# Attention values loaded to stepped partitions of SBUF, and the last strided values loaded into the key tiles

## The chip, the cores and the metric

The kernel runs on 1 core of a Trainium2 chip. The metric is device time of one execution in microseconds (us). TensorE (PE) multiplies, VectorE (DVE), ScalarE (ACT) and GpSimd (POOL) do the rest, and SyncE's queue (SP) issues nearly all transfers, in the order in which they are written.

## The reference

A sparse attention over `q`, `k`, `v` of 8 batches, 8 heads, 576 rows and 64 columns, and a soft mixture of experts behind it:

```
scores = q @ k.T / 8
heads 0..3: keep 0 <= row - key < 32              (local)
heads 4..7: keep key <= row, key % 32 == row % 32 (strided)
x = softmax(scores) @ v, reshaped to 4608 x 512
logits = x @ phi                                  (32 slots)
slot_in  = softmax(logits, over rows).T @ x
slot_out = relu(slot_in @ w1[e]) @ w2[e]          (8 experts, 4 slots each)
out = softmax(logits, over slots) @ slot_out
```

All is float32. The three attention inputs are 28.3 MB, the two weight tensors 33.6 MB, the output 9.4 MB.

## The kernel before

**Sets.** The attention runs over nine sets. Eight are the batches, without their first 64 rows; the set called B gathers those first 64 rows of all batches and is the fifth in order (`SETS`). In a set the four local heads and the four strided heads are handled as pairs: `a` is which pair, `j` which head of the pair. One set is some 60 small steps, each with a name in the text `ASEQ` (lines 38 to 44). An entry such as `AVs0:3` says that in iteration `it` the step is written for set `it - 3`; `A` or `D` behind it puts a copy on ACT or DVE. So ASEQ is a software pipeline five stages deep: with it every engine's order, and the order on SP's queue, are set by hand, and no scheduler changes them.

**Names of steps.** `LKl LQl LKs LQs` load keys and queries of the local and strided heads into the four tiles `ld[x][i]` (512 KB each), `LDr` loads the first key rows into `rest`. `TlK TlQ TsK TsQ Tr` transpose them on PE into PSUM; `lK lQ sK sQ lrK srK` copy them to `kbl`, `ql`, `kbs`, `qs`. `SL`, `SS` are the score products, `mxl`/`mxs` row maxima, `sbl`/`sbs` the subtraction, `exl`/`exs` the exponential, `sml`/`sms` sums and reciprocals, `nms` the scaling of the strided P. `PTl`, `PTs` transpose P; `ePTl`, `ePTs` copy it out of PSUM; `AVl`, `AVs` multiply it with the values; `X`, `XB`, `LG` transpose the result and make logits; `bm dex dT SI acc` fold the set into the running softmax over rows. `W` loads one weight buffer of 512 KB.

**Values.** A product with the values contracts over 128 partitions: both pairs `a` at once, 64 partitions each, and the zeros of the other pair keep them apart. `load_v1` (line 180) fetches the local heads in two transfers, pair 0 to partitions 0 to 63 and pair 1 to 64 to 127, in runs of 256 bytes. `make_v2` (line 202) makes a copy shifted by 32 keys on POOL, in four copies of 32 partitions. `load_vs` (line 190) fetches the strided heads, 32 partitions at 4 or 68 onwards in runs of 4 KB, and 4 more partitions in a small transfer. P is written to match: `(a, key)` down the partitions. Each tile of values exists once, so a load waits until the products of the set before have read it.

**PSUM.** Steps on PE that fill two banks (`T`, `SL`, `SS`, `PT`, `AV`, `X`, `XB`) take turns in three double banks (`pair2`, line 116): a step waits until what stood there three steps earlier has been read.

**The end of the attention.** Of the 64 weight pieces 24 have buffers of their own. The rest go where an attention tile has had its last use (`alias`, line 218; `freed`, line 270), and later into weight buffers that have been multiplied. For the last set (number 8) V1 and VS are written right behind the last `AVl` and `AVs` of set 7 (lines 570 to 592). Behind the attention, `cf` (constants, line 593) is fetched on ACT's queue, then follow slot inputs, the two expert layers (`h`, `so`) and the output (`o`) with its stores.

Of the kernel before, what the change touches and what calls it, by code (L numbers as in the profile page):

```python
# [22 lines left out]
G = 16  # L23
# [9 lines left out]
NWX = 3  # L33
# [13 lines left out]
def shape_constants():  # L47
# [25 lines left out]
    cf = np.concatenate([ident, same, stack, np.ones((128, 1), np.float32)], 1)  # L73
# [4 lines left out]
def tile_sparse_attention_soft_moe(  # L78
# [26 lines left out]
    ident = const.tile([P, 128], F32, name="ident")  # L105
# [44 lines left out]
    pl = fix.tile([P, 16, 64], F32, name="pl")  # L150
    psd = fix.tile([P, 8, 2, 64], F32, name="psd")
# [4 lines left out]
    pt = work.tile([P, 2, 512], F32, name="pt")  # L156
# [4 lines left out]
    for t in (v1, vs, v2, psd, pts):  # L161
        nc.gpsimd.memset(t, 0.0)
# [27 lines left out]
    def load_vs(b):  # L190
        rows = vs.rearrange("p j g d -> p j (g d)")
        for a in range(2):
            if b < B:
# [3 lines left out]
                continue  # L197
            for j in range(2):
                nc.sync.dma_start(out=rows[64 * a + 4:64 * a + NI, j],
                                  in_=v[:, 4 + 2 * a + j, 0:AUX].rearrange("b (i g) d -> b i (g d)", g=G))  # L200

    def make_v2(i):

        a, y = divmod(i, 2)
        r = 64 * a
        if y == 0:
            nc.gpsimd.tensor_copy(out=v2[r + 32:r + 64, a], in_=v1[r:r + 32, a, :, 1:9])  # L207
        else:
            nc.gpsimd.tensor_copy(out=v2[r:r + 32, a], in_=v1[r + 32:r + 64, a, :, 0:8])  # L209
# [8 lines left out]
    alias = [(ld[x][i].rearrange("p a x -> p (a x)"), {("TlK", "TlQ", "TsK", "TsQ")[2 * x + i]})  # L218
# [7 lines left out]
    alias += [(flat(vs, "p j g d -> p (j g d)", x), {f"AVs{y}" for y in range(4)}) for x in (0, 1024)]  # L226
    alias += [(flat(pl, "p g x -> p (g x)", 0), {"PTl"}), (flat(psd, "p g a x -> p (g a x)", 0), {"PTs"})]
# [162 lines left out]
    def row_sub(b, x):  # L390
        m = stats(b, "mx", x)
        if x == 1:
            nc.vector.tensor_tensor(out=probs(1), in0=scores(b, 1), in1=bc(m, NI), op=ALU.subtract)
            return

        nc.vector.tensor_tensor(out=pl.rearrange("p g (r n) -> p g r n", n=TN),
                                in0=bt[b]["sl"].rearrange("p j (g n r) -> p (j g) r n", n=TN, r=8),
                                in1=m.rearrange("p a g -> p (a g)").unsqueeze(2).unsqueeze(3).to_broadcast([P, 16, 8, TN]),
                                op=ALU.subtract)

    def row_exp(b, x):
# [9 lines left out]
    def nms(b):  # L411
        nc.vector.tensor_tensor(out=probs(1), in0=probs(1), in1=bc(stats(b, "rz", 1), NI), op=ALU.mult)

    def PT(b, x):
        ps = bt[b]["pt"] = pair2(f"pt{b}{x}")
        for g in range(8):
            nc.tensor.transpose(out=ps[:, g // 4, 128 * (g % 4):128 * (g % 4) + 128],  # L417
                                in_=(pl[:, 2 * g:2 * g + 2] if x == 0 else psd[:, g]).rearrange("p a k -> p (a k)"), identity=ident)
# [18 lines left out]
    def ePTs(b, a, cp):  # L437

        d = slice(64 * a, 64 * a + 64)
        cp(out=pts[d, a].rearrange("p j g x -> p (j g x)"), in_=bt[b]["pt"][d].rearrange("p j x -> p (j x)"))  # L440

    def AVs(b, e, w):
# [71 lines left out]
    def emit_acc(cols, ps, al):  # L514
# [6 lines left out]
    nc.scalar.dma_start(out=ident, in_=cfd[:, 0:128])  # L521
# [24 lines left out]
        "ePTl": lambda b, cp: cp(out=two(pt, 512), in_=two(bt[b]["pt"], 512)),  # L546
# [23 lines left out]
    after, left = {"AVl": "V1", "AVs": "VS"}, {"AVl": 2, "AVs": 4}  # L570

    done, asked = set(), 0
    for it in range(min(x[1] for x in todo), NV + max(x[1] for x in todo)):
        for name, stage, cp in todo:
            b = it - stage
            if not 0 <= b < NV or b == NV - 1 and name in after.values():
# [5 lines left out]
            if b == NV - 2 and name[:3] in after:  # L582
                left[name[:3]] -= 1
                if not left[name[:3]]:
                    steps[after[name[:3]]](NV - 1)
                    asked += 1
            asked += b == NV - 2 and name == "VS"
            if b == NV - 1:
                done.add(name)
            for x in [x for x in alias if x[1] <= done and asked > 1]:  # L590
                alias.remove(x)
                freed(x[0])
    nc.scalar.dma_start(out=cf, in_=cfd[:, 128:289])
# [148 lines left out]
    def emit_ct(vb):  # L742
# [36 lines left out]
    held = [n for n, x in enumerate(order) if x.tensor in (ld[0][0].tensor, ld[0][1].tensor)]  # L779
# [91 lines left out]
```

## Time and profile before

| | us |
|---|---|
| three runs | 284.42, 287.0, 291.0 (median 287.0) |
| the profiled execution, whole | 285.93 |
| its span, first to last instruction | 284.1 |
| TensorE busy | 232.5 |
| VectorE busy | 170.5 |
| ScalarE busy | 149.6 |
| GpSimd busy | 50.9 |

The span is what the views below divide; 1.8 us of the profiled execution lie outside it. Busy shares are means over a long attention part (to about 215 us) and an expert part, which have different limits.

### The profile page before, as it was taken

Reading aid. Unit: us, or ns where it says so; the run is one execution under the profiler, and the core shown is the slowest. Engines: PE = TensorE matmul, PEld = TensorE weight load, DVE = VectorE, ACT = ScalarE, POOL = GpSimd, SP = SyncE. Lnnn points to the kernel's source line nnn. Section 1 sums busy time; section 2 is a strip of 40 time slices with the busy share of each in tenths; the row PEclk is TensorE's granted clock in tenths of the full one; section 3 lists DMA queues with packets and bytes.
Section 4 is the critical chain, followed back from the end, with each engine's and each line's share of the span. In section 5 each row is a group of like instructions: output and inputs, shape, how many; then the busy total and the mean of one; then the engine's idle time right before and its main releaser. Section 6 shows DMA issues by size and latency. Waiting matters only on the chain.

```text
span 284.1 us, 8914 instructions
## 1 busy us (share of the span) xinstructions
PE 232.5 (82%) x3841; PEld 167.1 (59%) x3841; DVE 170.5 (60%) x309; ACT 149.6 (53%) x270; POOL 50.9 (18%) x48
## 2 busy tenths in 40 slices
PE   7997899899897899899898899971263999999800
PEld 3675686686685777686685677761241523566700
DVE  5389477587485577587576578851022175688810
ACT  3877686585873676865675677441020011277700
POOL 9205023032023032041023023141000020000000
PEclk9999999999999999999999999997586699999975
DMA  7999999797599998989999997899999399999997
GB/s 204 337 228 315 251 205 281 255 252 224 200 183 293 259 232 264 216 205 250 229 197 278 238 165 219 172 389 316 239 266 357 148 267 352 348 353 366 315 350 243
DMA packets 65416, 74.28 MB, mean 261 GB/s; under 512 B 24288, under 2 KB 50272, under 8 KB 65376
## 3 DMA queue, kind: packets, MB, share of 16 engines
q1 hardware_dynamic: 64416, 73.41, 96.1%
q8 instruction: 30, 0.49, 0.8%
q10 hardware_dynamic: 960, 0.30, 0.4%
q14 instruction: 10, 0.08, 0.1%
HBM read 64.26 MB, written 9.44 MB: 259 GB/s over the span
## 4 chain that ended last, share of the span: by engine, by line
PE 39%; DMA 39%; SPq 11%; ACT 2%; DVE 1%; issue 1%; POOL 0%; DVEq 0%; ACTq 0%; POOLq 0%
DMA vs<-in_v_dram 10%; DMA ld<-in_k_dram 9%; DMA rest<-in_k_dram 8%; DMA ld<-in_q_dram 7%; SPq L258 6%; PE h L691 5%; PE so L787 5%; PE as L281 5%; PE t L294 3%; PE o L815 3%; DMA v<-in_v_dram 3%; PE lg L281 3%; PE pt L417 2%; DMA kbl<-in_cf_dram 2%; PE ss L281 2%; PE al L281 2%
## 5 line engine op out<-in xcount | busy, mean ns | idle before, releaser
L294 PE MATMUL t<-ident,ld 128*128 128x128 f32 x288 | 40.9, 279 | 12.4 <-DMA ld<-in_k_dram 6.4
L294 PEld LDWEIGHTS t<-ident,ld 128*128 128x128 f32 x288 | 31.0, 140 | 23.9 <-issue 7.1
L207 POOL COPY v<-v 32x1024 f32<-32x1024 f32 x18 | 18.8, 1044 | 138.2 <-DMA v<-in_v_dram 127.5
L281 PE MATMUL as<-pts,vs 128*64 128x64 f32 x576 | 22.2, 234 | 10.3 <-DMA vs<-in_v_dram 10.3
L281 PEld LDWEIGHTS as<-pts,vs 128*64 128x64 f32 x576 | 19.7, 147 | 13.8 <-issue 13.4
L440 ACT COPY pts<-pt 64x1024 f32<-64x1024 f32 x18 | 18.1, 1007 | 16.7 <-PE pt L417 16.5
L310 ACT COPY kbl<-t 64x512 f32<-64x512 f32 x27 | 15.7, 581 | 17.3 <-PE t L294 17.0
L552 ACT COPY xt<-as 128x512 f32<-128x512 f32 x18 | 9.7, 589 | 25.2 <-PE as L281 25.2
L313 ACT COPY ql<-t 64x512 f32<-64x512 f32 x36 | 20.9, 580 | 3.6 <-PE t L294 2.7
L432 DVE TENSOR_TENSOR xn<-al,rz 128x512 f32<-128x512 f32 x18 | 11.6, 686 | 18.3 <-PE al L281 18.0
L209 POOL COPY v<-v 32x1024 f32<-32x1024 f32 x18 | 20.8, 1157 | 1.5 <-DMA v<-in_v_dram 0.6
L281 PE MATMUL al<-v,pt 128*32 128x128 f32 x576 | 19.9, 275 | 1.2 <-POOL v L207 1.1
L281 PE MATMUL sl<-kbl,ql 128*32 128x128 f32 x576 | 19.9, 276 | 0.1
L300 DVE COPY qs<-t 128x1024 f32<-128x1024 f32 x9 | 11.0, 1222 | 13.6 <-PE t L294 13.6
L303 ACT COPY kbs<-t 64x1024 f32<-64x1024 f32 x18 | 18.1, 1008 | 0.3
L281 PEld LDWEIGHTS al<-v,pt 128*32 128x32 f32 x576 | 15.2, 109 | 5.1 <-issue 3.6
L281 PEld LDWEIGHTS sl<-kbl,ql 128*32 128x32 f32 x576 | 14.8, 110 | 5.2 <-issue 4.9
L388 DVE TENSOR_REDUCE mx<-sl 128x16 f32<-128x1024 f32 x9 | 11.0, 1223 | 10.1 <-PE sl L281 10.1
L545 ACT COPY xt<-x 128x1024 f32<-128x1024 f32 x9 | 9.1, 1012 | 14.9 <-PE x L455 14.9
L478 DVE TENSOR_REDUCE bm<-lg 128x1 f32<-128x128 f32 x9 | 2.6, 284 | 19.3 <-PE lg L281 19.1
L281 PE MATMUL ss<-kbs,qs 128*32 128x72 f32 x576 | 14.0, 234 | 0.0
L281 PE MATMUL lg<-xt,phs 128*32 128x128 f32 x288 | 12.0, 287 | 1.4 <-ACT xt L552 1.4
(164 smaller groups left out, 436.5 us busy)
## 6 DMA issues: line engine op xcount, KB each, us to landing
wb<-in_moe_w_dram SPq DMA_DIRECT2D x41, 512.0 KB
ld<-in_k_dram SPq DMA_DIRECT2D x32, 256.0 KB
ld<-in_q_dram SPq DMA_DIRECT2D x32, 256.0 KB
v<-in_v_dram SPq DMA_DIRECT2D x16, 288.0 KB
vs<-in_v_dram SPq DMA_DIRECT2D x16, 256.0 KB
ld<-in_moe_w_dram SPq DMA_DIRECT2D x4, 512.0 KB
out_dram<-wb SPq DMA_DIRECT2D x4, 512.0 KB
v<-in_moe_w_dram SPq DMA_DIRECT2D x3, 512.0 KB
```

Of the source, the lines that this page charges most:

```text
L207: nc.gpsimd.tensor_copy(out=v2[r + 32:r + 64, a], in_=v1[r:r + 32, a, :, 1:9])
L209: nc.gpsimd.tensor_copy(out=v2[r:r + 32, a], in_=v1[r + 32:r + 64, a, :, 0:8])
L258: nc.sync.dma_start(out=buf, in_=w1[4 * g + e, 128 * c:128 * c + 128, :])
L281: nc.tensor.matmul(out=out, lhsT=lhsT, rhs=rhs, start=start, stop=stop, skip_group_check=True)
L294: nc.tensor.transpose(out=tp[:, a, P * n:P * n + P], in_=src[:, a, P * n:P * n + P], identity=ident)
L303: cp(out=kbs[r, y].rearrange("p n (j r) -> p n j r", j=2)[:, :, :, AR:PN], in_=tv[r].rearrange("p n (r j) -> p n j r", j=2))
L310: cp(out=kbl[d, e, a].rearrange("p n (j r) -> p n j r", j=2)[:, :, :, AR:PN], in_=tp[r, a].rearrange("p (n r j) -> p n j r", n=4, j=2))
L313: cp(out=ql[d, :, 32 * e:32 * e + 32].rearrange("p t (n r) -> p t n r", n=4), in_=tp[r, a].rearrange("p (n t r) -> p t n r", n=4, r=8))
L432: nc.vector.tensor_tensor(out=xn[:, 0].rearrange("p r (a j d) -> p j r a d", a=2, j=2)[:, j], in0=bt[b]["al"][:, j].rearrange("p (r a d) - ...
L440: cp(out=pts[d, a].rearrange("p j g x -> p (j g x)"), in_=bt[b]["pt"][d].rearrange("p j x -> p (j x)"))
L691: nc.tensor.matmul(out=ph[x][32 * e:32 * e + 32, :], lhsT=sit[:, c, 32 * (4 * g + e):32 * (4 * g + e) + 32], rhs=wts[16 * g + 4 * c + e][: ...
L787: nc.tensor.matmul(out=pos[x][32 * e:32 * e + 32, 0:256], lhsT=hts[g][:, c, 32 * e:32 * e + 32], rhs=wt[:, 256 * e:256 * e + 256], start=( ...
```

## The change

- Values of the local heads go to every second partition: pair 0 to 0, 2, 4, ... and pair 1 to 1, 3, 5, ... The partition is then `(key, a)`, and `row_sub` writes P in that order (two halves `sbl0`, `sbl1`, one for each `a`). `make_v2` becomes two copies of 64 partitions.
- Strided values: one transfer for each `j` brings 32 rows of both pairs to 64 even partitions (a row's pair is four partitions on from the row before it), a small one brings the first 4 rows to 8 odd partitions. P gets a compact tile `psc`, and `nms` writes it spread out into `psd` in two instructions. `ePTs` now copies all 128 partitions and multiplies by a 0/1 column (`own_a`), where before it copied 64 into a tile with zeros.
- `ePTl` copies back into `pl`, the tile of P itself; the tile `pt` is gone. The tail has two extra weight buffers, not three.
- The last set's strided values are loaded into `ld[0][0]` and `ld[0][1]`, the key and query tiles of the local heads, as soon as `TlK` and `TlQ` of that set are done. `V1` of the last set still waits for `AVl` of set 7.
- ASEQ is another text: order, stages and ACT/DVE choices differ; SP's loads have other places.

The core of the diff (left out: index plumbing of tiles that are only renamed, and the constants):

```diff
-NWX = 3
+NWX = 2
-    "srK0:2A LDr:1 sK1:2A kp1:4D kp0:4A VS:3 dex:4 LQl:1 LQs:1 PTs:3 dT:4 eXB:4D ePTs0:3A mxl:2 edT:4D AVl0:3 "
-    "sbl:2 alx:4 z:4 LKs:1 SI:4 TlK:1 ePTs1:3A acc:4 lK2:1A AVl1:3 SS0:2 nl0:3 V1:2 lK1:1A lK3:1A SS1:2 exl:2 "
...
+    "bm:4 kp0:4A dex:4 eXB:4A dT:4 sms:3 AVl1:3 lrK2:2D lrK3:2D lQ3:2A V1:2 lrK0:2D edT:4D lrK1:2D lQ1:2A alx:4 "
+    "LDr:1 nms:3 TsK:2 VS:3 SI:4 W2:2 z:4 lQ2:2A LQs:1 lQ0:2A nl1:3 nl0:3 V21:2 sK0:2A acc:4 SL0:2 sK1:2A SL1:2 "
+    "PTs:3 mxl:2 LQl:1 ePTs0:3A SS0:2 sbl1:2 ePTs1:3A sbl0:2 SS1:2 X:3 exl:2 TlK:1 mxs:2 lK1:1A sbs:2 Tr:1 AVs0:3 "
+    "lK0:1A LKs:1 AVs1:3 W3:2 lK2:1A W1:2 eX:3D AVs2:3 LGl:3 AVs3:3 PTl:2 lK3:1A sml:2 eAVs0:3A ePTl:2D TsQ:1 "
+    "srK0:1D eAVs1:3A exs:2 LGs:3 XB:3 V20:2 sQ:1A kp1:3D srK1:1D TlQ:1 AVl0:2 LKl:0 "
...
-            out = v1[64 * a:64 * a + 64, a]
+            out = v1[a::2, a]
...
+    vs_of = [[vs[:, j] for j in range(2)]] * (NV - 1) + [[ld[0][i].rearrange("p a (g d) -> p (a g) d", d=D) for i in range(2)]]
...
-                src = v[b, 4 + 2 * a:6 + 2 * a].rearrange("j (i g) d -> i j (g d)", g=G)
-                for lo, hi in ((4, NI), (0, 4)):
-                    nc.sync.dma_start(out=rows[64 * a + lo:64 * a + hi], in_=src[lo:hi])
+        src = v[b, 4:8].rearrange("(a j) (i g) d -> i a j (g d)", j=2, g=G)
+        for j in range(2):
+            for rows, lo, hi in ((slice(0, P, 2), 4, NI), (slice(1, P, 16), 0, 4)):
+                nc.sync.dma_start(out=to[j][rows].rearrange("p g d -> p (g d)"), in_=src[lo:hi, :, j])
...
-            nc.gpsimd.tensor_copy(out=v2[r + 32:r + 64, a], in_=v1[r:r + 32, a, :, 1:9])
+            nc.gpsimd.tensor_copy(out=v2[64:128], in_=v1[0:64, :, :, 1:9])
...
-        nc.vector.tensor_tensor(out=probs(1), in0=probs(1), in1=bc(stats(b, "rz", 1), NI), op=ALU.mult)
+        for out, lo, hi in ((psd.rearrange("p g (k a x) -> p x g a k", a=2, x=2)[:, 0], 4, NI),
+                            (psd.rearrange("p g (k a x) -> p x g a k", a=2, x=16)[:, 1], 0, 4)):
+            nc.vector.tensor_tensor(out=out, in0=pv[:, :, :, lo:hi], in1=bc(t, hi - lo), op=ALU.mult)
...
-        d = slice(64 * a, 64 * a + 64)
-        cp(out=pts[d, a].rearrange("p j g x -> p (j g x)"), in_=bt[b]["pt"][d].rearrange("p j x -> p (j x)"))
+        out, src, own = pts[:, a].rearrange("p j g x -> p (j g x)"), two(bt[b]["pt"], 512), own_a[:, a:a + 1]
+        if cp is ACT:
+            nc.scalar.activation(out=out, in_=src, func=AF.Copy, scale=own)
...
-    after, left = {"AVl": "V1", "AVs": "VS"}, {"AVl": 2, "AVs": 4}
+    asks = {("TlK", "TlQ"): (NV - 1, "VS"), ("AVl0", "AVl1"): (NV - 2, "V1")}
```

Two places show how instructions move. The first is SP's queue at the end of the attention. `ld_105` to `ld_108` are the four key and query tiles, `wb` weight buffers, `v_114` and `vs` the values, and loads from `moe_w` are weights. Before (the `...` stands for loads of `ql`, `kbl`, `qs`):

```order
L258 DMA wb_101<-in_moe_w_dram 128x1024
L196 DMA vs<-in_v_dram 32x2x1024
...
L185 DMA v_114<-in_v_dram 64x18x64 x2
L258 DMA ld_105<-in_moe_w_dram 128x1024
...
L264 DMA kbs<-in_moe_w_dram 128x4x256 x2
L196 DMA vs<-in_v_dram 32x2x1024
L196 DMA vs<-in_v_dram 4x2x1024
...
L264 DMA pl<-in_moe_w_dram 128x4x256
```

And with the change:

```order
L265 DMA wb_101<-in_moe_w_dram 128x1024
L209 DMA ld_105<-in_v_dram 64x1x1024
L209 DMA ld_105<-in_v_dram 8x1x1024
L209 DMA ld_106<-in_v_dram 64x1x1024
L209 DMA ld_106<-in_v_dram 8x1x1024
L191 DMA v_114<-in_v_dram 64x18x64 x2
L209 DMA vs<-in_v_dram 64x1x1024
...
L265 DMA ld_107<-in_moe_w_dram 128x1024
```

The last strided values (to `ld_105` and `ld_106`) now stand ahead of every weight that follows the 24th, and ahead of set 7's own strided values; before, ten weight loads stood between them and the last `v_114`.

The second place is PE's queue in one full iteration, from `X` on. Before:

```order
L455 MATMUL x_538<-ident,xn 128x128 x8
L323 MATMUL tr_548<-ident,rest 128x4x16 x4
L294 MATMUL t_555<-ident,ld_106 128x128 x8
L294 MATMUL t_567<-ident,ld_108 128x128 x8
L281 MATMUL as_580<-pts,vs 64x32x2 x24
L281 MATMUL lg_614<-xt,phs 32x128 x8
L281 MATMUL as_580<-pts,vs 64x32x2 x8
L417 MATMUL pt_641<-ident,pl 128x128 x8
L294 MATMUL t_653<-ident,ld_107 128x128 x8
```

With the change:

```order
L468 MATMUL x_835<-ident,xn 128x128 x8
L301 MATMUL t_845<-ident,ld_105 128x128 x8
L330 MATMUL tr_858<-ident,rest 128x4x16 x4
L288 MATMUL as_863<-pts,vs 64x32x2 x24
L288 MATMUL lg_895<-xt,phs 32x128 x8
L288 MATMUL as_863<-pts,vs 64x32x2 x8
L427 MATMUL pt_912<-ident,pl 128x128 x8
L301 MATMUL t_928<-ident,ld_108 128x128 x8
```

The transposes of loaded tiles (`t`) that stood side by side are spread over the iteration, and the kinds and counts of PE's instructions in an iteration are the same.

## Rows read from the trace of the kernel before

**Rows 1.** The page: engines' busy time, and the SP queue's share of 16 engines.

```profile
PE 232.5 (82%) x3841; PEld 167.1 (59%) x3841; DVE 170.5 (60%) x309; ACT 149.6 (53%) x270; POOL 50.9 (18%) x48
...
q1 hardware_dynamic: 64416, 73.41, 96.1%
```

**Rows 2.** Stages: us, busy of PE, PEld, DVE, ACT, POOL, clock, DMA share, GB/s.

```profile
35.00:55.00 20.00, 18.89 (x364) 14.51 (x364) 13.61 (x23) 14.03 (x24) 4.23 (x4) 1.00 1.00 245
55.00:75.00 20.00, 20.00 (x379) 15.92 (x378) 15.58 (x26) 14.35 (x26) 4.56 (x4) 1.00 0.89 235
...
185.00:205.00 20.00, 7.18 (x123) 5.98 (x117) 4.68 (x10) 4.22 (x8) 4.16 (x4) 0.75 1.08 312
```

**Rows 3.** Chain in order of time (start, us, what): one set, first and last rows.

```profile
52.90 1.81 PE ss L281 x58
...
72.02 1.87 PE ss L281 x58
```

**Rows 4.** Timeline of PE (start, us, instruction): first SS of sets 0, 1 and 8.

```profile
15.26 0.29 PE L281 MATMUL ss<-cb 128*128 128x288 bf16 x1
31.98 0.30 PE L281 MATMUL ss<-cb 128*128 128x288 bf16 x1
177.68 0.30 PE L281 MATMUL ss<-cb 128*128 128x288 bf16 x1
```

**Rows 5.** DMA from 76 to 86 us in 40 slices: share, GB/s.

```profile
DMA  5555555899999999999998799999999999889999
GB/s 197 197 189 197 197 197 197 284 259 246 240 160 146 176 158 165 139 209 167 181 213 99 84 167 238 251 180 169 136 81 129 145 188 253 200 229 360 328 360 442
```

**Rows 6.** DMA from 86 to 96 us, GB/s in 40 slices.

```profile
GB/s 442 393 410 377 410 377 426 361 401 459 402 328 205 123 164 180 82 180 213 147 180 131 197 229 238 230 156 139 213 229 352 311 164 115 156 213 336 352 328 238
```

**Rows 7.** DMA from 98.5 to 101.5 us (values of set B), GB/s in 40 slices.

```profile
GB/s 304 263 188 195 103 130 126 130 171 150 222 178 174 191 102 140 126 126 147 123 154 99 150 130 123 150 120 154 123 150 102 123 137 143 102 130 137 184 174 195
```

**Rows 8.** Timeline, end of the attention (last bracket: idle before, and what ended it).

```profile
191.88 2.47 SPq L196 DMA_DIRECT2D vs<-in_v_dram  x4
...
204.01 2.83 PE L281 MATMUL as<-pts,vs 128*64 128x64 f32 x48 [10.25 <-DMA vs<-in_v_dram]
210.71 0.29 DVE L478 TENSOR_REDUCE bm<-lg 128x1 f32<-128x128 f32 x1 [18.16 <-PE lg L281]
211.53 0.34 ACTq L593 DMA_DIRECT2D kbl<-in_cf_dram  x1
211.70 1.22 DVE L548 COPY xn<-xb 128x1024 f32<-128x1024 f32 x1 [0.37 <-PE xb L462]
218.41 0.55 PE L624 MATMUL mrg<-kbl,phs 1*128 1x1 f32 x2 [3.02 <-DMA kbl<-in_cf_dram]
```

**Rows 9.** Timeline of SP, expert part.

```profile
226.20 22.30 SPq L264 DMA_DIRECT2D wb<-in_moe_w_dram  x17
...
276.63 2.73 SPq L829 DMA_DIRECT2D out_dram<-pts  x2
```

**Rows 10.** DMA from 220 to 284 us, GB/s in 40 slices.

```profile
GB/s 413 253 36 0 77 262 238 277 333 367 348 348 349 348 346 349 348 348 356 338 349 360 382 371 371 357 353 350 337 241 308 371 356 344 340 344 341 319 254 38
```

**Rows 11.** Instructions by shape: names, shapes, count | busy us, mean ns | idle.

```profile
L388 DVE TENSOR_REDUCE mx<-sl 128x16 f32<-128x1024 f32 x9 | 11.0, 1223 | 10.1 <-PE sl L281 10.1
L396 DVE TENSOR_TENSOR pl<-sl,mx 128x1024 f32<-128x1024 f32 x9 | 11.0, 1217 | 0.1
L408 DVE TENSOR_SCALAR rz<-rz 128x16 f32<-128x16 f32 x18 | 6.5, 362 | 0.6
...
L440 ACT COPY pts<-pt 64x1024 f32<-64x1024 f32 x18 | 18.1, 1007 | 16.7 <-PE pt L417 16.5
L545 ACT COPY xt<-x 128x1024 f32<-128x1024 f32 x9 | 9.1, 1012 | 14.9 <-PE x L455 14.9
...
L207 POOL COPY v<-v 32x1024 f32<-32x1024 f32 x18 | 18.8, 1044 | 138.2 <-DMA v<-in_v_dram 127.5 <-PE as L281 10.2
```

**Rows 12.** Timeline of DVE: the same L408 without a copy on POOL beside it.

```profile
80.61 0.17 DVE L408 TENSOR_SCALAR rz<-rz 128x16 f32<-128x16 f32 x1
```

More of the change, by code (lines that the diff above doesn't have):

```diff
@@ L72, in shape_constants @@
     stack = (r[:, None] % 32 == np.arange(32)[None, :]).astype(np.float32)
-    cf = np.concatenate([ident, same, stack, np.ones((128, 1), np.float32)], 1)
+    own = np.stack([(r % 4 == 2 * a) | (r % 32 == 1 + 16 * a) for a in range(2)], 1).astype(np.float32)
+    cf = np.concatenate([ident, own, same, stack, np.ones((128, 1), np.float32)], 1)
     return cb, np.ascontiguousarray(cf, np.float32)
@@ L160, in tile_sparse_attention_soft_moe @@
         nc.vector.memset(t, 0.0)
-    for t in (v1, vs, v2, psd, pts):
+    for t in (v1, vs, v2, psd):
         nc.gpsimd.memset(t, 0.0)
@@ L216, in tile_sparse_attention_soft_moe @@
     own = list(wbufs)
-    alias = [(ld[x][i].rearrange("p a x -> p (a x)"), {("TlK", "TlQ", "TsK", "TsQ")[2 * x + i]})
+    alias = [(ld[x][i].rearrange("p a x -> p (a x)"), {("TsK", "TsQ")[i]} if x else {f"AVs{y}" for y in range(4)})
              for x in range(2) for i in range(2)]
@@ L225, in tile_sparse_attention_soft_moe @@
     alias += [(flat(v1, "p a j s d -> p (a j s d)", 1152), {"AVl0", "AVl1"})]
-    alias += [(flat(vs, "p j g d -> p (j g d)", x), {f"AVs{y}" for y in range(4)}) for x in (0, 1024)]
-    alias += [(flat(pl, "p g x -> p (g x)", 0), {"PTl"}), (flat(psd, "p g a x -> p (g a x)", 0), {"PTs"})]
+    alias += [(flat(vs, "p j g d -> p (j g d)", x), {"vs"}) for x in (0, 1024)]
+    alias += [(flat(pl, "p g k a -> p (g k a)", 0), {"AVl0", "AVl1"}), (flat(psd, "p g x -> p (g x)", 0), {"PTs"})]
     alias += [(flat(xt, "p a t -> p (a t)", 0), {"LGs", "XB"})]
@@ L437, in ePTs @@
     def ePTs(b, a, cp):
-        d = slice(64 * a, 64 * a + 64)
-        cp(out=pts[d, a].rearrange("p j g x -> p (j g x)"), in_=bt[b]["pt"][d].rearrange("p j x -> p (j x)"))
+        out, src, own = pts[:, a].rearrange("p j g x -> p (j g x)"), two(bt[b]["pt"], 512), own_a[:, a:a + 1]
+        if cp is ACT:
+            nc.scalar.activation(out=out, in_=src, func=AF.Copy, scale=own)
+        else:
+            nc.vector.tensor_scalar_mul(out, src, own)
     def AVs(b, e, w):
@@ L545, in tile_sparse_attention_soft_moe @@
         "eX": lambda b, cp: cp(out=two(xt, 512), in_=two(bt[b]["x"], 512)),
-        "ePTl": lambda b, cp: cp(out=two(pt, 512), in_=two(bt[b]["pt"], 512)),
+        "ePTl": lambda b, cp: cp(out=pl.rearrange("p g k a -> p (g k a)"), in_=two(bt[b]["pt"], 512)),
         "ePTs0": lambda b, cp: ePTs(b, 0, cp), "ePTs1": lambda b, cp: ePTs(b, 1, cp),
@@ L575, in tile_sparse_attention_soft_moe @@
             b = it - stage
-            if not 0 <= b < NV or b == NV - 1 and name in after.values():
+            if not 0 <= b < NV or b == NV - 1 and name in ("V1", "VS"):
                 continue
@@ L581, in tile_sparse_attention_soft_moe @@
                 steps[name](b)
[L582 to L593, printed above, removed]
+            done.add((name, b))
+            for first, (n, load) in asks.items():
+                if load not in asked and {(x, n) for x in first} <= done:
+                    steps[load](NV - 1)
+                    asked.add(load)
+            if {(f"AVs{y}", NV - 2) for y in range(4)} <= done:
+                done.add(("vs", NV - 1))
+            if len(asked) == 2 and ("VS", NV - 2) in done:
+                for x in [x for x in alias if {(y, NV - 1) for y in x[1]} <= done]:
+                    alias.remove(x)
+                    freed(x[0])
+    nc.scalar.dma_start(out=cf, in_=cfd[:, 130:291])
     st["m"], st["z"] = bt[NV - 1]["ngm"], bt[NV - 1]["zs"]
@@ L774, in tile_sparse_attention_soft_moe @@
     emit_h(1)
-    held = [n for n, x in enumerate(order) if x.tensor in (ld[0][0].tensor, ld[0][1].tensor)]
+    held = [n for n, x in enumerate(order) if x.tensor in (ld[0][0].tensor, ld[0][1].tensor, ld[1][0].tensor)]
     free = [wts[j] for j in list(range(64 - NL + 3, NL)) if not 32 - NWX <= j < 32 and seq.index(j) not in held]
```

69 lines of the change are left out of this document (35 added, 34 removed), and 3 rows, old and new, of the table ASEQ.

## The prediction

> **What bounds the kernel now.** I read the page first: TensorE is busy for 82% of the span, and the packets of SP's queue fill 96% of the 16 DMA engines' time [rows 1]. Two resources look full, so the stages come next. In the middle of the attention PE is busy 18.9 of 20 us with a DMA share of 1.00, and then 20.0 of 20 with a share of 0.89 [rows 2]: the bound changes hands. The chain of waits gives PE's own floor. From the `ss` products of one set, at 52.90, to those of the next, at 72.02, the chain has PE rows only [rows 3], so a set in which PE never waits takes 19.1 us. What sets really take stands in the timeline: the first `ss` of set 0 is at 15.26, of set 1 at 31.98, of set 8 at 177.68 [rows 4]. The first interval is 16.7 us while the pipeline fills; the other seven take 145.7, or 20.8 each. So 1.7 us a set is not PE's; DMA holds it.
>
> The rates say which transfers are slow. The lowest rates come with the engines as busy as ever: 80 to 250 GB/s, mostly under 200, at a share of 0.8 to 1.0 behind the slice that reads 284 [rows 5], where the local values arrive. Keys, queries and weights run at 360 to 460 GB/s (the first eleven slices of rows 6); the strided values behind them run at 80 to 240. The first rows of `v` for set B, 256 byte runs to 64 neighbouring partitions, run at about 140 [rows 7]. One transfer steps partitions already: the keys and queries of set B go to every second partition, on 8 engines by their shape, and read 197 GB/s at a share of 0.5 [rows 5], half the engines at full speed each.
>
> The last thing to see is the end of the attention. The last strided values are issued at 191.88, and PE waits 10.25 us for them until 204.01 [rows 8]; that stage has a clock of 0.75 [rows 2]. Behind the attention the queue is full again: from 226.20, when the first used weight buffers are refilled, to the last stores [rows 9] it moves 17 pieces of 0.52 MB and 9.4 MB of output at about 345 GB/s, with few dips [rows 10].
>
> **DMA in a set.** Each set moves 3.67 MB of keys, queries and three weights; at 390 GB/s that is 9.4 us. The first key rows (0.13 MB, 64 neighbouring partitions, taken at 197) cost 0.7. The period of 20.8, which DMA fills, leaves 10.7 us for 1.18 MB of values: 110 GB/s. With the change the strided values have the run length of the weights, all 16 engines and stepped partitions. I take 390 GB/s for their two large transfers (1.4 us), and 0.7 for the two small ones, which use 4 engines. The local values keep runs of 256 bytes, and no row shows that size on stepped partitions. Their bounds are 140 GB/s (4.2 us, nothing gained over rows 7) and 390 (1.5 us); I take 200, or 3.0, nearer to the slow row since the run length is the same. So values cost 5.1 us in place of 10.7 and a set's DMA is 15.2 (13.7 to 16.4), below PE's 19.1. Gathering at half speed is thus enough to hand the bound to PE.
>
> The rule behind it is in the Trainium skill, SBUF — State Buffer, Door 1: The DMA port swizzle: partitions 0 to 63 reach only 8 of 16 ports, with 196 GB/s measured against 328 for 128 partitions. Rows 5 and 6 agree in kind. By that ratio alone the 10.7 us would become an estimated 6.4, and a set's DMA 16.5, still under PE.
>
> **PE, DVE and ACT in a set.** PE issues the same kinds and counts, so 19.1 stays. Added on DVE: `sbl` in two halves of 512 (1217 ns for 1024 now [rows 11]; some 0.15 more), a second small `nms` (0.2), and the copies `eX` and `ePTl` (1.2 each) come to DVE while `sQ` and `eXB` leave it: about 14 us a set. `ePTs` on ACT covers 128 partitions in place of 64 with the same 1024 elements each, 1.01 us either way (1007 against 1012 [rows 11]). Both engines keep 4 to 5 us to spare under 19.1. The tightest place I find by laying the new order out with these durations is `X`: it takes the PSUM buffer of `SL` and must wait for `mxl` (1.22) and both halves of `sbl` (about 1.4), 2.6 us, while PE has `PTs` and `SS` to do, 2.8 us. Such places may cost between 0 and 1 us a set; I take 0.2. Loads in SP's order come in time: `V1` can start some 1 us into an iteration and `VS` lands by 9, before `AVs` at 11; the copies on POOL (four of 1.04 now [rows 11], two of about 2.1 with the change) end by 12, before `AVl0` at 18. `V1` is moved ahead of set 1's queries at the start, which delays those by 3 us, while PE there is busy with `SL` and `SS` of set 0.
>
> **The sum**, on the span of 284.1 us:
>
> - Seven intervals at 19.3, not 20.8: -10.5 us. The second one lacks `SI`, which I leave as reserve. The fill (first interval 16.7) loses some waits; bounds 0 to 2.5, I take -1.5.
> - The wait for the last strided values: -10.25, since they go to tiles that are free when the last transposes of local keys and queries end, a full iteration before their products. PE then does not fall to 0.75 in the 6.7 us behind it: -1.7 (a quarter). What is late next is the plain chain of `nms`, `PTs`, `ePTs`, `AVs`, `LG`, about 19 us behind the last `SS`.
> - `cf` is issued on ACT behind `eXB`, which was on DVE: +1.8 (it left 0.8 us behind `bm` at 210.71, and took 6.7 to PE's start at 218.41 [rows 8]).
> - One weight buffer less in the tail: 18 pieces, not 17, in the queue at the end: 0.52 MB at 345 GB/s, +1.5.
> - The 22 weights that go to freed tiles need 11.5 MB at 350, 33 us, from about 161 to 194, before the first refill at about 205: 0 (0 to +3 if the transfers of values hold them up). That cover is nearly used up.
>
> 284.1 - 10.5 - 1.5 - 10.25 - 1.7 + 1.8 + 1.5 = 263.4 us of span. The profiled execution lasted 285.93, 1.8 more, so **265 us**; its time stands 1.1 below the median of 287.0, within its spread.
>
> **Rivals.**
>
> - *The loads gain nothing* (what limits them is the short run or the memory side, not the partitions, so the change does not do what it says). Then sets stay at 20.8 and only the end gains: 284.1 - 12 + 3.3 + 1.8 = 277 us. Against it: strided values have long runs and are as slow as short ones [rows 6, 7], and stepped loads run at full speed per engine [rows 5]. Chance 0.12.
> - *A chain on DVE and POOL takes the place of DMA.* A small VectorE operation takes 0.17 us alone [rows 12] and 0.36 in the mean [rows 11], so some wait for POOL's copies of 1.04 us. Copies of 2.1 would hold one of them up to twice as long, in `sml` or `sms`, on the way to `PTl` and `PTs`; with `X` as above a set takes 20.3 to 20.8 and the total is 272 to 276. For it: PE's slack in the new order is under 1 us at two places. Chance 0.15. The Trainium skill, SBUF — State Buffer, Who interferes with whom, says that the shared port is held for a whole instruction and the loser fully blocks; the 0.36 agrees.
> - *The fill and the end gain more*: DMA no longer delays the fill, the order has no stall, and `cf` finds an emptier queue (3 us, not 6.7). Then 7 x 0.2 + 1 + 3.7 less: 259 and, with `SI` missing in one interval, down to 255. Chance 0.15 beyond my likeliest range.
> - *Stepping slows short runs.* If transfers of values fall from 110 GB/s to half, they take 21.4 us, a set's DMA 31.5, and eight sets lose 12 us each: 362. This turns the sign from about 92 GB/s on: values then cost 12.8 us, a set 22.9, and 8 x 3.6 us use up the 28 gained. Against it is the 197 on 8 engines [rows 5]. Chance 0.04.
>
> The forecast itself, 259 to 270, has 0.54. **Range:** 255 to 277, from the third rival to the first; it leaves out the fourth and the edges. About 2% (5.7 us) is what a measurement here can tell from no change: faster means below 281, and all cases but the last and a part of the first two lie there. Chances: faster 0.91, within 2% 0.05, slower 0.04.
>
> **What would show it.** Right: `ss` to `ss` at 19 to 19.6 us with no waits of PE on `ld`; a DMA share clearly below 1 in the middle of the attention; no low stretches below 150 GB/s; `as` of the last set without a wait; stores ending as before, 50 to 60 us behind the first refill. Wrong: shares still at 1.0 with 20.8 a set (first rival); PE waiting for DVE or ACT by 1 us a set (second); or weights landing late in the expert part, so that the attention ends early and the stores do not.

## The result, and the profile after

| us | before | after |
|---|---|---|
| median of 4 runs | 288.12 (284.42 to 291.0) | 259.43 (258.48 to 259.56) |
| the profiled execution, its span | 285.93, 284.1 | 259.56, 257.4 |

The ratio is 0.907, with an interval of 0.899 to 0.915: faster by 9%. The forecast was 265 us with a range of 255 to 277.

The page of the changed kernel first: busy times and the share of SP's queue, to be held against [rows 1].

```profile
PE 228.6 (89%) x3841; PEld 165.4 (64%) x3841; DVE 167.6 (65%) x350; ACT 148.9 (58%) x247; POOL 43.6 (17%) x29
...
q1 hardware_dynamic: 64416, 73.41, 88.2%
```

The same 3841 matmuls, the same 64416 packets and 73.41 MB. PE now fills 89% of the span, and the queue's share fell from 96.1 to 88.2% although the span is shorter: the same bytes took less of the engines' time.

The stages of the attention, 20 us each (columns as in [rows 2]), and the whole of 35 to 155 us:

```profile
35.00:55.00 20.00, 19.98 (x402) 15.81 (x402) 14.38 (x29) 14.00 (x22) 3.81 (x2) 1.00 0.90 294
55.00:75.00 20.00, 19.99 (x400) 15.70 (x389) 14.62 (x30) 14.63 (x24) 3.80 (x2) 1.00 0.72 221
...
35.00:155.00 120.00, 119.45 (x2299) 94.13 (x2296) 86.83 (x173) 87.59 (x136) 22.77 (x12) 1.00 0.83 266
```

The long stretch of the kernel before, for comparison:

```profile
35.00:155.00 120.00, 111.83 (x2098) 86.40 (x2098) 82.92 (x137) 81.89 (x141) 26.35 (x24) 1.00 0.99 238
```

PE goes from 111.8 to 119.5 of 120 us, the DMA share from 0.99 to 0.83. The bound has changed hands: before, DMA had hardly any idle time in the attention and PE had; now it is the other way round.

PE's timeline, the first `ss` of sets 0, 1, 2 and 8, answers to [rows 4]:

```profile
15.19 0.30 PE L288 MATMUL ss<-cb 128*128 128x288 bf16 x1
...
29.14 0.29 PE L288 MATMUL ss<-cb 128*128 128x288 bf16 x1
...
49.02 0.29 PE L288 MATMUL ss<-cb 128*128 128x288 bf16 x1
...
164.35 0.29 PE L288 MATMUL ss<-cb 128*128 128x288 bf16 x1
```

From set 1 to set 8 there are now 135.2 us, or 19.3 a set; before they were 145.7, or 20.8.

DMA from 60 to 70 us in 40 slices of 0.25 us shows one load of values:

```profile
DMA  6555351100000000165999999999999798973978
GB/s 180 213 188 188 148 180 74 49 25 25 0 0 0 0 0 0 29 160 123 222 288 288 286 290 268 263 223 297 279 295 328 262 360 311 262 164 82 262 262 311
```

The queue runs dry for 1.5 us, since `V1` waits for `AVl1` on SP and everything written behind it waits too; then the local values come at 263 to 290 GB/s, in slices as long as those of [rows 5], where they came at 84 to 213.

The end of the attention, rows of PE, DVE, ACT and SP in order of time, answers to [rows 8] and [rows 9]:

```profile
180.47 1.69 PE L288 MATMUL as<-pts,ld 128*64 128x64 f32 x48 [0.72 <-DMA vs<-in_moe_w_dram]
185.44 0.28 DVE L491 TENSOR_REDUCE bm<-lg 128x1 f32<-128x128 f32 x1
186.40 0.34 ACTq L606 DMA_DIRECT2D kbl<-in_cf_dram  x1
191.90 0.34 PE L637 MATMUL mrg<-kbl,phs 1*128 1x1 f32 x1 [2.26 <-DMA kbl<-in_cf_dram]
199.41 24.20 SPq L271 DMA_DIRECT2D wb<-in_moe_w_dram  x18
```

The wait of 10.25 us for the last strided values is gone; 0.72 is left. This row puts it down to a weight load that has nothing to do with these products; the trace of `a_cf_early` below puts the same 0.72 down to ACT's copy of `pts`. The 48 products took 2.83 before and 1.69 now, and the granted clock from 170 to 185 us is 1.00, where before it was 0.75 from 185 to 205.

### The profile page after: what moved, and what is told of

The parts are those of the page before. It is cut to its first block, busy times and chain, and to the rows that moved or that the text cites. A ratio compares the mean times of both kernels' runs of the same rounds, so it can differ in the third digit from the quotient of the medians.

```text
span 257.4 us, 8952 instructions
## 1 busy us (share of the span) xinstructions
PE 228.6 (89%) x3841; PEld 165.4 (64%) x3841; DVE 167.6 (65%) x350; ACT 148.9 (58%) x247; POOL 43.6 (17%) x29
## 3 DMA queue, kind: packets, MB, share of 16 engines
q1 hardware_dynamic: 64416, 73.41, 88.2%
## 4 chain that ended last, share of the span: by engine, by line
PE 69%; DMA 12%; SPq 6%; ACT 3%; DVE 2%; issue 2%; DVEq 0%; ACTq 0%
PE t L301 10%; PE as L288 8%; PE al L288 6%; PE sl L288 6%; PE h L704 6%; PE so L800 6%; DMA vs<-in_v_dram 5%; PE pt L427 5%; PE lg L288 4%; PE o L828 4%; PE ss L288 3%; DMA vs<-in_moe_w_dram 3%; PE xb L475 3%; DMA kbl<-in_cf_dram 2%; SPq L209 2%; PE x L468 2%
## 5 line engine op out<-in xcount | busy, mean ns | idle before, releaser
L216 POOL COPY v<-v 64x2048 f32<-64x2048 f32 x9 | 17.1, 1900 | 126.2 <-DMA v<-in_v_dram 126.2
L451 ACT ACTIVATE pts<-pt,ident 128x1024 f32<-128x1024 f32 x18 | 19.1, 1114 | 22.7 <-PE pt L427 22.7
L317 ACT COPY kbl<-t 64x512 f32<-64x512 f32 x36 | 20.9, 579 | 7.9 <-PE t L301 7.3
L288 PE MATMUL as<-pts,vs 128*64 128x64 f32 x512 | 19.3, 225 | 1.6 <-DMA vs<-in_v_dram 1.6
L559 DVE COPY pl<-pt 128x1024 f32<-128x1024 f32 x9 | 11.0, 1218 | 15.0 <-PE pt L427 15.0
L288 PEld LDWEIGHTS as<-pts,vs 128*64 128x64 f32 x512 | 16.8, 138 | 4.3 <-issue 3.3
L288 PE MATMUL al<-v,pl 128*32 128x128 f32 x576 | 19.4, 275 | 0.0
L214 POOL COPY v<-v 64x2048 f32<-64x2048 f32 x9 | 17.0, 1893 | 0.5
L565 ACT COPY xt<-as 128x512 f32<-128x512 f32 x18 | 9.7, 589 | 12.8 <-PE as L288 8.0
L288 PEld LDWEIGHTS al<-v,pl 128*32 128x32 f32 x576 | 14.8, 109 | 2.5 <-issue 1.5
L288 PEld LDWEIGHTS ss<-kbs,qs 128*32 128x32 f32 x576 | 10.3, 110 | 3.1 <-issue 1.8
L828 PE MATMUL o<-rs,ct 128*128 128x256 f32 x72 | 11.1, 294 | 0.9 <-DVE rs L817 0.9
## 6 DMA issues: line engine op xcount, KB each, us to landing
v<-in_v_dram SPq DMA_DIRECT2D x16, 288.0 KB
```

Of the source, the lines that this page charges most:

```text
L214: nc.gpsimd.tensor_copy(out=v2[64:128], in_=v1[0:64, :, :, 1:9])
L216: nc.gpsimd.tensor_copy(out=v2[0:64], in_=v1[64:128, :, :, 0:8])
L288: nc.tensor.matmul(out=out, lhsT=lhsT, rhs=rhs, start=start, stop=stop, skip_group_check=True)
L317: cp(out=kbl[d, e, a].rearrange("p n (j r) -> p n j r", j=2)[:, :, :, AR:PN], in_=tp[r, a].rearrange("p (n r j) -> p n j r", n=4, j=2))
L451: nc.scalar.activation(out=out, in_=src, func=AF.Copy, scale=own)
L828: nc.tensor.matmul(out=pq[:, 256 * y:256 * y + 256], lhsT=cts[vb][:, 128 * (2 * (t % 2) + t // 2):128 * (2 * (t % 2) + t // 2) + 128], rhs ...
```

## The experiments

The kernel before was timed beside each of them; its own median moved between 285.3 and 289.1 from one comparison to the next, so ratios are compared, and 2 us between two of them tell nothing.

**One part alone, in the order of before.** The first kernel is the one before with its two loads of values on stepped partitions and nothing else.

```diff
-            out = v1[64 * a:64 * a + 64, a]
+            out = v1[a::2, a]
...
+            for j in range(2):
+                for rs, lo, hi in ((slice(0, P, 2), 4, NI), (slice(1, P, 16), 0, 4)):
+                    nc.sync.dma_start(out=rows[rs, j], in_=src[lo:hi, :, j])
```

> The kernel before, its order untouched, with both kinds of values loaded to stepped partitions as in the change (P keeps the old order, so values and P no longer match; only the time counts). Theory 1 (the slow loads held the sets): sets go from 20.8 us towards PE's 19.1 to 19.6, the wait at the end shrinks a little: 270 to 278 us. Rival (without the new order the faster loads help nothing): 283 to 288.

267.0 us (265.5 to 267.6), ratio 0.938 (0.931 to 0.945): more than expected. The stretch from 35 to 155 us, and PE at the last strided values:

```profile
35.00:155.00 120.00, 120.00 (x2351) 95.74 (x2346) 89.44 (x153) 90.93 (x156) 29.27 (x28) 1.00 0.84 267
```

```profile
182.86 0.45 PE L282 MATMUL as<-pts,vs 128*64 128x64 f32 x2 [6.97 <-DMA vs<-in_v_dram]
184.07 2.79 PE L282 MATMUL as<-pts,vs 128*64 128x64 f32 x46 [0.76 <-DMA vs<-in_v_dram]
```

PE is busy for the whole 120 us in the old order too. Stepping the partitions is all that it takes to hand the bound to PE (for the strided values it comes with another cut of the transfers, by head and not by pair; the two were not tried apart). The wait at the end is still there, at 7.0 and 0.8 us.

The second is the kernel before with the last strided values early in the key tiles, on neighbouring partitions.

```diff
+            if b == NV - 1 and name in ("TlK", "TlQ") and {"TlK", "TlQ"} <= done | {name}:
+                load_vs(SETS[b], True)
```

> The kernel before with one part of the change alone: the last set's strided values go to the two local key and query tiles as soon as their last transposes are done, to contiguous halves. Result unchanged. Theory 1: the wait of 10 us at the end and the low clock behind it go, 10 to 12 us less: 273 to 277 us. Rival (the expert part is bound by DMA, so an earlier end of the attention is given back): 283 to 288.

284.5 us (runs 286.0, 284.0, 285.0 and 277.4) beside 285.3: no gain that can be told. Three of the four runs lie in the range of the rival. The fourth can't be put down to the edit: `b_pe_more` below, which only adds work, has such a run too, at 280.6. PE's timeline, of the run with 286.0, says why the expected 10 to 12 us did not come:

```profile
196.44 2.03 PE L290 MATMUL al<-v,pt 128*32 128x128 f32 x32 [4.85 <-POOL v L216]
...
204.39 1.62 PE L290 MATMUL as<-pts,ld 128*64 128x64 f32 x48
```

`as` has no wait any more, but `al` ahead of it waits 4.85 us for POOL's copy of the last *local* values, which come late in the same slow queue. The wait has moved by one tile.

The third has both parts, still in the old order:

```diff
+            for j in range(2):
+                for rs, lo, hi in ((slice(0, P, 2), 4, NI), (slice(1, P, 16), 0, 4)):
+                    nc.sync.dma_start(out=vs_of[-1][j][rs].rearrange("p g d -> p (g d)"), in_=src[lo:hi, :, j])
```

> Both parts together in the old order of steps (values and P no longer match). Theory 1: the two gains add up to nearly the whole: 260 to 267 us. Rival (the new order carries a third or more of the gain): 268 or more.

257.6 us (256.4 to 258.9), ratio 0.905 (0.899 to 0.912). Stepping alone is worth 18 us, early values alone nothing that can be told, both 28: the second part gains 9 us once the loads are quick. These two parts make the whole gain.

**The order of the steps.** The change with the text `ASEQ` of before, the tile `pt` and a weight buffer less:

```diff
-NWBUF = 24
+NWBUF = 23
...
-    pt = pl.rearrange("p (j g) k a -> p j (g k a)", j=2)
+    pt = work.tile([P, 2, 512], F32, name="pt")
```

> The changed kernel with the old order of steps (the text ASEQ of before; sbl in its two halves, the shifted copies in two). P has its second tile pt back, and to make room one weight buffer is left out, 23 for 24, which by the queue at the end costs about 1.5 us. Result unchanged. Theory 1 (the loads and the early last values carry the gain, the new order nothing): 257 to 262 us. Rival (the new order is worth something once P is laid out anew): 264 or more.

260.8 us (259.8 to 261.9), ratio 0.910 (0.903 to 0.917), which overlaps that of the change. The new order is worth nothing that shows here. In the trace the last `bm` comes at 184.33, 1.1 us ahead of the change, and the span is 258.8, 1.4 behind it, with one weight buffer less.

**Undoing the stepping in the change.** Both loads of values to neighbouring partitions, all else as changed:

```diff
-            out = v1[a::2, a]
+            out = v1[64 * a:64 * a + 64, a]
...
-            for rows, lo, hi in ((slice(0, P, 2), 4, NI), (slice(1, P, 16), 0, 4)):
-                nc.sync.dma_start(out=to[j][rows].rearrange("p g d -> p (g d)"), in_=src[lo:hi, :, j])
+            for a in range(2):
+                for lo, hi in ((4, NI), (0, 4)):
+                    nc.sync.dma_start(out=to[j][64 * a + lo:64 * a + hi].rearrange("p g d -> p (g d)"), in_=src[lo:hi, a, j])
```

> The changed kernel, but both kinds of values are loaded to contiguous halves again (pair 0 at partitions 0 to 63, pair 1 at 64 to 127) while P keeps the new order; only the time counts, since values and P no longer match. Theory 1 (stepping made the loads fast enough to hand the bound to PE): a set's DMA rises by 4 to 6 us to 20 to 22, over PE's 19.2, so eight sets lose 1 to 3 us each: 268 to 282 us, with PE waiting for ld tiles. Rival (the new order of steps did it, DMA has slack either way): 258 to 263 us.

279.2 us (277.2 to 282.4), ratio 0.978 (0.971 to 0.985), inside what was expected. But the way it gets there is not quite the predicted one. PE's waits (us in total, times, longest), and the stretch from 35 to 155 us:

```profile
PE as L295 <- DMA vs<-in_v_dram: 10.8, 5, 3.3
```

```profile
35.00:155.00 120.00, 111.80 (x2050) 88.37 (x2050) 76.08 (x156) 77.59 (x124) 18.95 (x10) 0.94 0.87 238
```

PE is as short of work as before, yet DMA has 13% of its time left. So it isn't DMA's total alone that PE waits for: `V1` stands in SP's queue until `AVl1` is done, `VS` stands behind it, and `AVs` of the same iteration needs `VS`. One such wait, by windows (columns as in [rows 2]):

```profile
36.50:40.00 3.50, 3.50 (x64) 3.23 (x64) 0.00 (x0) 0.00 (x0) 0.00 (x0) 0.50 1.05 390
40.00:45.00 5.00, 5.00 (x63) 4.25 (x56) 1.99 (x5) 2.67 (x4) 0.00 (x0) 0.77 0.96 297
```

PE's wait of 3.27 us ends at 36.50. Then the granted clock is 0.50, the lower of its two levels (1.2 and 2.4 GHz), and 0.77 in the mean of the next 5 us: 3.5 x 0.5 + 5 x 0.23 = 2.9 us more. That set takes 25.3 us, from 28.76 to 54.05, 6.1 over an undisturbed one: the wait and the clock behind it.

If the place in the queue is what makes it dear, then `VS` ahead of `V1` should give most of it back, with the loads as slow as ever:

```diff
-    "bm:4 kp0:4A dex:4 eXB:4A dT:4 sms:3 AVl1:3 lrK2:2D lrK3:2D lQ3:2A V1:2 lrK0:2D edT:4D lrK1:2D lQ1:2A alx:4 "
-    "LDr:1 nms:3 TsK:2 VS:3 SI:4 W2:2 z:4 lQ2:2A LQs:1 lQ0:2A nl1:3 nl0:3 V21:2 sK0:2A acc:4 SL0:2 sK1:2A SL1:2 "
+    "bm:4 kp0:4A dex:4 eXB:4A dT:4 sms:3 AVl1:3 lrK2:2D lrK3:2D lQ3:2A VS:3 V1:2 lrK0:2D edT:4D lrK1:2D lQ1:2A alx:4 "
+    "LDr:1 nms:3 TsK:2 SI:4 W2:2 z:4 lQ2:2A LQs:1 lQ0:2A nl1:3 nl0:3 V21:2 sK0:2A acc:4 SL0:2 sK1:2A SL1:2 "
```

> Both kinds of values to contiguous halves in the changed kernel (279 us), with the strided values written ahead of the local ones on SP's queue (values and P no longer match). If the slow loads cost time by their place in the queue, the strided values being awaited first: 262 to 270. If they cost it by filling DMA: 276 to 283.

267.5 us (266.0 to 269.3), ratio 0.933 (0.924 to 0.942). PE's waits for `vs` fall from 10.8 us to one, and the clock of 35 to 155 us from 0.94 to 0.99:

```profile
PE as L295 <- DMA vs<-in_v_dram: 2.3, 1, 2.3
```

```profile
35.00:155.00 120.00, 118.16 (x2261) 93.02 (x2260) 87.56 (x170) 86.05 (x134) 24.23 (x13) 0.99 0.91 261
```

So in the new order 12 of the 20 us that slow loads cost are their place in the queue; what the other 8 are was not taken apart.

One load at a time. Local values on neighbouring partitions (the first line pair of the diff of both):

> The changed kernel with only the local values loaded to contiguous halves (values and P no longer match for the local heads). Theory 1: their 0.59 MB fall from about 280 GB/s to about 140, 2 us more a set; DMA is then at about 18 to 19, just under PE's 19.2: 259 to 266 us. Rival (order alone): 258 to 261. Second rival (POOL's shifted copies then come late for the products): over 266, with PE waiting for POOL.

261.6 us (260.0 to 261.9), ratio 0.917 (0.912 to 0.923), which touches that of the change: about 2 us, not settled.

Strided values on neighbouring partitions (its second part):

> The changed kernel with only the strided values loaded to contiguous halves, the last set's too (values and P no longer match for the strided heads). Theory 1: 1.5 to 2.5 us of DMA more a set, under PE's floor: 259 to 265 us, some of it at the end, where two loads are awaited. Rival (order alone): 258 to 261.

270.3 us, but 266.0 to 272.8 from run to run, so no ratio is given; some 7 us or more above the change. The expectation was too low: strided values are the ones awaited, and what delays them PE pays in full (it waits 4.5 us in two places, the longer 2.4), while local values have POOL's copies and half an iteration ahead of their products.

**Is it the step, or that the stepped load reaches both halves of the partitions?** Local values to every second partition of one half, in four transfers of 32:

```diff
+                for h in range(2):
+                    nc.sync.dma_start(out=v1[64 * a + h:64 * a + 64:2, a], in_=src[32 * h:32 * h + 32])
```

> The changed kernel; the local values of a pair go to every second partition, but of one half of the partitions (0, 2, ... 62, then 1, 3, ... 63; 64 on for the other pair), in two transfers of 32 partitions each (values and P no longer match). If it is the half of the partitions that makes the load slow: about 140 GB/s in the stretches of short runs as in the kernel before, 260 to 264 us. If it is neighbouring partitions: about 280 GB/s as in the change, 258.5 to 260.5.

263.2 us (259.5 to 264.9), ratio 0.910 (0.900 to 0.920), and the time can't tell. The rates can. DMA from 103 to 111 us in slices of 0.2 us, where the same set's values arrive. With the change:

```profile
GB/s 225 191 216 271 289 284 266 289 288 280 286 142 124 133 123 205 205 225 164 225 246 184 225 184 348 287 287 307 348 369 277 246 348 328 184 164 266 184 287 348
```

Every second partition of one half:

```profile
GB/s 133 216 265 199 236 256 201 193 238 224 170 111 82 123 164 164 205 205 205 184 184 348 102 266 287 348 451 205 266 215 195 215 430 348 277 236 277 307 358 287
```

Neighbouring partitions (local values on halves):

```profile
GB/s 0 0 0 44 224 247 279 292 256 172 158 163 155 201 182 178 177 252 91 161 27 143 123 225 348 307 205 348 348 369 266 266 195 246 225 287 225 266 246 236
```

The load comes at 266 to 289 in its main part with the change, and at 193 to 265 stepped in one half. On neighbours it has two parts: five slices at 224 to 292, as quick as with the change, and then 155 to 201. Neither theory's number came: stepping in one half gives a rate between the two. The Trainium skill, SBUF — State Buffer, Door 1: The DMA port swizzle, gives partitions 0 to 63 half of the ports whichever of them are used, so by it the last two would be alike; the trace does not agree.

The packets of these three loads, from the same traces, say more. A packet of 256 bytes took, in the mean of the first half of the load's packets and of the second, 18 and 20 ns with the change, 18 and 21 stepped in one half, and 19 and 33 on neighbours. So neighbours are slow only in the second half, about where the second of their two transfers comes, and stepping in one half takes this away. Its rate is still lower than with the change; SP took 2.69 us to issue its four transfers, and 1.40 to issue two. This speaks against the half as the cause; but four short transfers may also overlap less than two long ones, so whether the step or the smaller transfers make the packets quick stays open.

**Is PE the bound now?** `TsQ` transposes each block twice, first on the change, then on the kernel before:

```diff
+                for _ in range(2 if x == 1 and i == 1 else 1):
```

> The changed kernel with the eight transposes of TsQ issued twice, about 1.0 us more of PE in each of nine sets; the result is unchanged. Theory 1 (PE is the bound of the attention): 8.5 to 9.5 us more, 268 to 269. Rival (another engine or DMA is, and PE's busy time hides waits): under 4 us more, below 263.

264.8 us (264.3 to 265.4), ratio 0.930 (0.924 to 0.935): 5.3 us more by the medians and 6.4 by the ratios, not the 8.5 to 9.5 expected. PE's timeline, sets 1 to 3:

```profile
28.98 0.29 PE L288 MATMUL ss<-cb 128*128 128x288 bf16 x1
...
49.02 0.29 PE L288 MATMUL ss<-cb 128*128 128x288 bf16 x1
...
69.06 0.29 PE L288 MATMUL ss<-cb 128*128 128x288 bf16 x1
```

Five of the seven intervals grew by 0.87 us, all of what was added to PE in a set (its busy time rose by 7.4 us in nine sets, or 0.82). The other two, 19.88 us long with the change, grew by 0.16 only. In those two PE waits for strided values in the trace of the change; the first such wait is

```profile
33.30 0.33 PE L288 MATMUL as<-pts,vs 128*64 128x64 f32 x2
34.05 1.58 PE L288 MATMUL as<-pts,vs 128*64 128x64 f32 x46 [0.42 <-DMA vs<-in_v_dram]
```

Neither this run nor `a_cf_early` below, which has the attention of the change up to the last set, has such a wait in its trace. In that of `a_cf_early` the first `ss` of sets 1 and 8 are 133.78 us apart, where the change took 135.21:

```profile
28.69 0.29 PE L288 MATMUL ss<-cb 128*128 128x288 bf16 x1
...
162.47 0.29 PE L288 MATMUL ss<-cb 128*128 128x288 bf16 x1
```

Against that trace all seven intervals grew, by 6.1 us together (139.89 with the doubled transposes), and the stretch from the last `ss` to `bm` did not (20.19 and 20.25). So PE is the bound in all seven sets when the strided values come in time. Less came than was expected because a set has 0.82 us more and not 1.0, and because seven sets pay and not nine.

> The kernel before with the eight transposes of TsQ issued twice, 0.85 us more of PE in each set; result unchanged. In the changed kernel this cost 5.3 us. If the sets of before are held by DMA: 0 to 3 us more. If PE holds them as it does in the changed kernel: 5 us more or above.

288.0 us (289.6, 288.0, 288.0 and 280.6) beside 285.3: the scatter is as large as the effect looked for. It settles nothing.

**The wait for `cf` that is left.** `cf` is fetched one step earlier, behind `exl` of the last set:

```diff
+            if name == "exl" and b == NV - 1:
+                nc.scalar.dma_start(out=cf, in_=cfd[:, 130:291])
```

> The changed kernel with the constants cf fetched behind the exponential of the last set's local scores, 20 us earlier on ACT's queue, so that PE's wait of 2.3 us for them behind the attention goes. Result unchanged. If the way through the first expert layer sets the end: 2 us less, 257 to 258. If the queue of weights and stores sets it: 259 to 260, the same.

261.2 us (258.7 to 262.2), ratio 0.910 (0.904 to 0.916): nothing. Rows of PE and SP:

```profile
187.50 0.38 PE L638 MATMUL mrg<-kbl,phs 1*128 1x1 f32 x2 [0.65 <-DVE phs L634]
...
195.38 1.98 SPq L265 DMA_DIRECT2D wx<-in_moe_w_dram  x2
197.47 27.39 SPq L271 DMA_DIRECT2D wb<-in_moe_w_dram  x18
```

`mrg` starts 4.4 us earlier and no longer waits for `cf`; 2.8 of the 4.4 are there at `bm` already (182.66, not 185.44), without the waits for strided values named above. The first refill is issued 1.9 us earlier, but the 18 refills take 27.4 us in place of 24.2 and end later. That the queue of weights and stores sets the end agrees with this, and with its share of 1.00 from the first refill on in the trace of the change. But this run does not show it, since its edit holds up the same queue: `cf` lies in a part of `kbl`, and among SP's own waits stands

```profile
SPq L265 <- DMA kbl<-in_cf_dram: 8.5, 1, 8.5
```

The weights for `kbl` are issued at 172.07 and not at 165.36, and the last two of the 22 weights (`wx`) right ahead of the first refill, by 197.4 and not 192.7. No version tried is told apart from the change as a faster one.

## Why the prediction was right

Its terms, each between two rows of the traces, in us (the sum of the measured ones is 284.1 - 257.4):

| stretch | predicted | before | after | measured |
|---|---|---|---|---|
| seven intervals, `ss` of set 1 to 8 | -10.5 | 145.70 | 135.21 | -10.5 |
| start to `ss` of set 1 (fill) | -1.5 | 31.98 | 29.14 | -2.8 |
| last `ss` to `bm` (wait for `vs`, clock) | -11.95 | 33.03 | 21.09 | -11.9 |
| `bm` to `mrg` (`cf` behind `eXB`) | +1.8 | 7.70 | 6.46 | -1.2 |
| `mrg` to the first refill | 0 | 7.79 | 7.51 | -0.3 |
| first refill to the end (one piece more) | +1.5 | 57.90 | 57.99 | +0.1 |
| sum | -20.7 | | | -26.7 |

- **The mechanism held.** A set without a wait takes 19.17 us, PE's floor as read from [rows 3], and the two largest terms came to within 0.1 us. Stepping the loads alone showed the first (PE 120.00 of 120), the doubled transposes that PE is the bound behind it.
- **That they came so close is in part luck.** The prediction added 0.2 us a set for the buffer of `X` and had `VS` land 2 us ahead of `AVs`. In the trace PE waits for the strided values of two of the seven sets (19.88 us each) and for those of set 7 behind the last `ss` (0.78 us, in the second term). In the trace of `a_cf_early`, with none of these waits, the two terms are -11.9 and -12.8.
- **DMA in a set** was put at 15.2 us (13.7 to 16.4); share 0.83 of 19.3 is 16.0. The traces' packets from `ss` of set 1 to that of set 8, added up by size and given for one set in us of all 16 engines, say where the time lies. The local values' runs of 256 bytes took 4.9 before and 2.65 after, near the 3.0 of the prediction. Runs of 4 KB (weights, strided values) took 6.8 after, where its terms make 6.1. Runs of 2 KB (keys, queries, first key rows) took 6.1 after, as in its terms, but 7.4 before, though the change leaves their destinations alone: so part of the 10.7 us that the prediction put down to values was keys and queries that ran slower beside them. Since PE has the bound this moved nothing.
- **The fill, `cf` and the tail** were all too dear, by 1.3, 3.0 and 1.4 us: this is nearly the whole miss of 6.0. `cf` was issued 1.0 us behind `bm`, where 0.8 had been before, and took 5.5 us to the use of it, not 6.9 (the prediction read 6.7). The prediction had the first two in the rival "the fill and the end gain more" (255 to 259). The time came out at that rival's edge, but only partly by its terms: it had 3.7 for `cf` and 1.4 from the sets, where 3.0 and nothing came, and it did not have the tail; the interval without `SI` took 18.78, 0.4 less than the others. In the tail the queue moved the piece more in the same 58 us, at 327 GB/s in place of 318; no run was made on that alone.
- **The 22 weights** cost nothing, as said: SP has issued them all by 192.7 us, 6.7 us ahead of the first refill. How little cover that is shows in `a_cf_early`, where a wait of 8.5 us in the queue used it up.
- **What the prediction told too simply:** it set DMA's total against PE's total in a set. In the old order that is right (share 0.99). In the new order slow loads cost 20 us while DMA has time left, 12 of them through the place of `VS` behind `V1` in SP's queue, with the clock behind the waits.
- **And it gave the early last values their 10.25 us as a term of their own.** Alone they are worth nothing that can be told, since the local values are late next; with quick loads they are worth 9. The sum was right only because the change does both.
- **Rivals.** *The loads gain nothing*: refuted by the rates and by stepping alone. *A chain on DVE and POOL*: POOL's copies of 64 partitions took 1.90 us each and not 2.1, and PE waited for none of them; the L408 of [rows 11], 0.36 us in the mean, is L413 now and takes 0.175:

```profile
L413 DVE TENSOR_SCALAR rz<-rz 128x16 f32<-128x16 f32 x18 | 3.1, 175 | 0.6
```

  In the mean it is as short as it was alone in [rows 12], so longer copies did not hold it longer. *Stepping slows short runs*: the opposite. There the prediction has 28 us to use up, but its own sum gains 20.7; the sign would turn at about 100 GB/s and not at 92.
- **A sign that did not come:** slices below 150 GB/s are still there, 82 at 69 us and 123 to 142 behind the values in the window of 103 to 111.

## What to carry to other kernels

When DMA looks full, read the rate of each kind of transfer: a slow kind at a full share can hold the bound with few bytes, and here other destination partitions for a quarter of a set's bytes were worth 18 us. Before taking a wait away, ask which transfer of the same queue is late next; the same edit was worth nothing that could be told alone and 9 us with quick loads. A load that is awaited in the iteration in which it is issued pays for what stands ahead of it in its queue, even where the engines have time left.

## What the runs showed of the hardware that was not expected

- Runs of 256 bytes came at 263 to 290 GB/s on 64 stepped partitions. On 64 neighbours, with the same packets, they began as quick (224 to 292) and went on at 155 to 201, and a packet's mean time rose from 19 to 33 ns. The Trainium skill, DMA: Bandwidth & Descriptors, Specifications, asks for 512 bytes or more for the line rate; that these loads did not reach the 360 to 460 of keys, queries and weights agrees.
- Slow loads slowed others. Runs of 2 KB, whose destinations no run changed, took 7.4 us of all 16 engines a set in the kernel before and 6.0 with the values stepped (`b_step`); in the new order the two are 6.4 (`a_both_halves`) and 6.1.
- A wait of PE of 3.27 us was followed by a granted clock of 0.50 for 3.5 us and cost 6.1 us in all; in the kernel before, 10.25 us were followed by products of 2.83 us in place of 1.69.
- Some kernels scatter from run to run (284 to 291 before, 266 to 273 with the strided loads undone, 259.5 to 264.9 with local values stepped in one half); the change stayed within 258.5 to 259.6. Why is open.
